# Two Fourier filters and two token MLPs on one core: the filter stage's last groups from one written list, more buffers and a sooner split

## The chip, the cores and the metric

The kernel runs on one core of one Trainium2 chip. Its time is the device time of one execution in microseconds (us); shown is the median of three runs. A core has five engines with an instruction stream each: TensorE (PE) for matmuls, VectorE (DVE), ScalarE (ACT) and GpSimd (POOL) for elementwise work, and SyncE (SP), which here only issues DMA transfers. An engine works through its own stream in order; engines wait for each other by semaphores. Matmuls write into PSUM, everything else lies in SBUF.

## The reference

Two kinds of layers alternate, A, B, A, B, each on the layer-normalised input and with a residual. A multiplies the 2-D spectrum with a complex filter, B is an MLP over the tokens:

```python
def A(x, w_r, w_i):                  # x: (1, 2048, 640)
    X = rfft2(x) * (w_r + 1j * w_i)  # (1, 2048, 321)
    return irfft2(X, s=(2048, 640))
def B(x, w1, b1, w2, b2):            # F = 1728
    h = layernorm(x)
    u = gelu(einsum("bsd,sf->bdf", h, w1) + b1)
    return (einsum("bdf,fs->bds", u, w2) + b2).transpose(0, 2, 1)

x = x + A(layernorm(x)); x = x + B(layernorm(x))
x = x + A(layernorm(x)); x = x + B(layernorm(x))
```

## The kernel before

The transforms are matmuls with tables of sines and cosines. To keep precision at f16 speed most operands are split into a high f16 part and a low f16 part (what the high one leaves over), and a product is three matmuls: high by high, high by low, low by high. So most stages have this shape: PE writes PSUM, ACT writes the high part from it, DVE or POOL the low part, PE reads both.

One pass over both layers is called a stage pair here; the program makes two of them. In each stand, in this order: a1, the filter stage (this case's subject); a2, the inverse transform of the rows, residual and the next layernorm; then the two products of the MLP, b1st and b2nd. What a1 hands to a2 is Y, split into Yh and Yl. A tile of a2 is 16 matmuls (`id_mm`), each of which reads rows of every group: the first two read Yh, the third Yl. ACT evicts the tile as "eh".

The filter stage works on 16 groups of columns, g = 0 to 15. A group passes through these steps; in the list of the change they go by the short names given here:

- d (`dstage`): 16 matmuls of 160 or 161 columns into a PSUM tile (24 for the first two groups); ph and pl: its high part (ACT) and low part (DVE).
- s (`s2stage`): 12 matmuls of 321 columns. For the last group it is done in three column blocks of 128, 128 and 65 columns, 12 matmuls each.
- ta, tb (`filtered`): two multiplies on DVE from that PSUM tile, with the filter's values w (a tile that SP loads per group) and a scale sx; each is 128 x 642.
- sa, sb (`sums`): the difference and the sum that finish the complex product, 128 x 321 each, on POOL.
- xh (ACT) and xl (POOL): the split of the product into f16; uh and ul (`twice`, ACT) copy 63 of its columns to columns 321 to 383, since the inverse transform reads a mirrored spectrum.
- i (`is2stage`): 36 matmuls of 64 rows and 128 columns in three column blocks, first those that read xh; Yh (ACT) and Yl (DVE, two instructions) split the result.

PSUM has four slots, and every `big()` takes the next one in turn; a group takes three (d, s, i). xh and xl lie in three buffers, `xs[g % 3]`. What runs when is written out by hand: all engine instructions go through a small wrapper (line 50, so every row of the profile has L50), which keeps them in program order on their engine while `self.pin` is set. DMAs on SP are not held this way; a scheduler places them.

The loop over g = 0 to 14 does d of group g + 1, i of group g - 3, s of group g, then xh, uh, xl of group g - 2, ta, tb, sa, sb of group g - 1, ph and pl of group g + 1, Yh and Yl of group g - 3, ul of group g - 2. Three other things are laid into it. `wsplit` splits the first weight tile of the MLP, in quarters: its high parts wh (ACT) at the end of g = 9 to 12, its low parts wl (DVE) behind pl at g = 10 to 13. The load of w of group g + 2 stands at the end of each g. And in the first of the two passes the bounds on the weights are worked out (`scan1`, `scale_b`, `scale1`), with two small matmuls by ones; each of them takes a PSUM slot of its own in `total`:

```python
        ps = at() if at else self.big()[:, 0, :n]
        self.PE.matmul(ps, self.ones, b, start=True, stop=True)
```

What is left of groups 13 to 15 after the loop is a sequence of its own. There the last group's product is worked on in two parts of columns, "a" (0 to 255) and "b" (256 to 320): ta15a, tb15a, ta15b, tb15b in a row on DVE; the sums of part a on POOL, of part b on DVE; xl15a and xl15b on DVE; the i of group 15 in two PSUM tiles. From its top:

```python
        h = self.big()
        for lt in range(3):
            s2mm(h, pp[k + 1], lt)
        xhi(k - 1, every, ta[k - 1])
        twice(k - 1, 0)
        xlo(k - 1, every, ta.pop(k - 1))
```

## Time and profile before

| | us |
|---|---|
| median of three runs | 1035.72 (1034.92 to 1037.0) |
| the profiled execution | 1035.4 |
| its span, first to last instruction | 1033.6 |
| PE busy | 988.2 (96%) |
| DVE busy | 723.8 (70%) |
| ACT busy | 571.1 (55%) |
| POOL busy | 264.1 (26%) |
| first filter stage, from 59.86 to 134.80: PE, DVE busy | 68.56, 62.34 |
| second filter stage, from 565.67 to 636.59: PE, DVE busy | 67.23, 59.06 |
| mean granted clock of TensorE | 0.977 |

How to read it: the span is cut from one profiled execution, and the rows of a timeline give the start, the duration of one instruction, its engine, the line, the operation, what it writes and reads with shapes and types, how many stand in a row, and in brackets for how long the engine had been idle before and which instruction released it. PE, DVE, ACT and POOL are engines, SPq is the queue that SP feeds. The granted clock is the share of full speed at which TensorE was allowed to run; 0.50 makes a matmul twice as long.

### The profile page before, as it was taken

The numbers are of one execution on the slowest core, as the hardware profiler recorded it, in microseconds if no ns is written. First come the engines' busy times: TensorE is split into PE (matmuls) and PEld (weight loads), VectorE is DVE, ScalarE is ACT, GpSimd is POOL, SyncE is SP. The second block draws the span as 40 slices with busy tenths as digits, with TensorE's granted clock in tenths as the row PEclk, the third lists the DMA queues.
The fourth block names the chain that finished last, engine by engine and source line by source line (L and its number), as shares of the span: only waits on it lengthen the run. The fifth ranks groups of instructions, "written<-read, shape, count | busy, mean of one in ns | idle before, by whom it ended". The sixth has DMA issues, their size and how long they took to land.

```text
span 1033.6 us, 20949 instructions
## 1 busy us (share of the span) xinstructions
PE 988.2 (96%) x8379; PEld 736.3 (71%) x8379; DVE 723.8 (70%) x1424; ACT 571.1 (55%) x874; POOL 264.1 (26%) x436
## 2 busy tenths in 40 slices
...
GB/s 226 276 181 173 101 161 220 210 84 93 80 78 75 71 238 153 135 130 123 124 64 95 195 132 120 199 186 197 129 84 82 72 107 78 140 153 174 163 44 52
DMA packets 55738, 139.48 MB, mean 135 GB/s; under 512 B 6461, under 2 KB 12249, under 8 KB 55641
## 3 DMA queue, kind: packets, MB, share of 16 engines
...
## 4 chain that ended last, share of the span: by engine, by line
PE 75%; DVE 10%; POOL 6%; ACT 4%; issue 3%; DMA 1%; SPq 0%; POOLq 0%; ACTq 0%; DVEq 0%
PE ps L50 75%; DVE st L50 2%; POOL ta L50 2%; DVE f L50 2%; POOL xt L50 1%; DVE xt L50 1%; DVE s1l L50 1%; DVE hl L50 1%; POOL xl L50 1%; ACT xh L50 1%; ACT eh L50 1%; DVE el L50 1%; POOL r L50 1%; DMA xt<-x 1%; POOL eo L50 1%
## 5 line engine op out<-in xcount | busy, mean ns | idle before, releaser
L50 PEld LDWEIGHTS <-wh 128*128 128x128 f16 x2992 | 289.7, 98 | 113.2 <-issue 1.7
L50 PEld LDWEIGHTS <-wl 128*128 128x128 f16 x1616 | 157.9, 98 | 62.2 <-DVE wl L50 0.7
L50 PE MATMUL ps<-hh,wh 128*128 128x320 f16 x896 | 186.6, 299 | 0.7 <-ACT hh L50 0.7
L50 PE MATMUL ps<-hl,wh 128*128 128x320 f16 x896 | 184.6, 299 | 0.0
L50 PE MATMUL ps<-hh,wl 128*128 128x320 f16 x832 | 171.5, 299 | 0.4 <-DVE wl L50 0.4
L50 DVE SCALAR_TENSOR_TENSOR wl<-raw,s,wh 128x1024 f16<-128x1024 f32 (+2 forms) x88 | 105.3, 1200 | 87.6 <-ACT wh L50 87.6
L50 PE MATMUL ps<-uh,wl 128*128 128x320 f16 x448 | 133.1, 299 | 0.0
L50 PE MATMUL ps<-ul,wh 128*128 128x320 f16 x448 | 133.0, 299 | 0.0
L50 ACT ACTIVATE wh<-raw,s 128x1024 f16<-128x1024 f32 (+2 forms) x92 | 94.7, 1047 | 69.0 <-PE ps L50 62.3
L50 PE MATMUL ps<-uh,wh 128*128 128x320 f16 x416 | 124.3, 299 | 0.0
L50 ACT ACTIVATE junk<-raw 128x896 bf16<-128x896 f32 (+1 forms) x60 | 59.6, 993 | 44.7 <-DMA raw<-w 44.5
L50 PE MATMUL ps<-tDi,Yh 128*128 128x322 f16 x320 | 73.3, 306 | 0.8 <-ACT Yh L50 0.8
L50 POOL TENSOR_TENSOR r<-v,mh 128x1 f32<-128x1 f32 x64 | 37.4, 584 | 133.2 <-DVE nm L50 122.8
L50 PE MATMUL ps<-u,wo 128*128 128x320 f16 x504 | 69.9, 299 | 0.0
L50 DVE TENSOR_TENSOR f<-eo 128x256 f32<-128x256 f32 (+1 forms) x124 | 39.0, 367 | 38.8 <-POOL eo L50 38.2
L50 PEld LDWEIGHTS <-wo 128*128 128x128 f16 x504 | 49.3, 98 | 19.1
L50 POOL TENSOR_TENSOR xt<-xt,ec 128x320 f32<-128x320 f32 x64 | 52.4, 840 | 40.8 <-DVE xt L50 40.5
L50 DVE BATCH_NORM_STATS2 st<-xt 128x6 f32<-128x320 f32 x126 | 55.2, 480 | 6.3 <-DMA xt<-x 5.3
L50 ACT ACTIVATE z<-xt,nb,r 128x640 f32<-128x640 f32 x31 | 28.5, 919 | 55.8 <-POOL z L50 43.5
L50 PE MATMUL ps<-ph,tS 128*128 128x321 f16 (+2 forms) x288 | 58.0, 286 | 0.1
L50 PE MATMUL ps<-tM,f 128*128 128x128 f32 x160 | 37.0, 396 | 22.1 <-DMA xt<-x 12.3
L50 PE MATMUL ps<-tDi,Yl 128*128 128x322 f16 x192 | 56.9, 305 | 1.1 <-DVE Yl L50 1.0
...
## 6 DMA issues: line engine op xcount, KB each, us to landing
...
```

The source lines that it names most:

```text
L50: i = f(*a, **k)
```

## The change

The steps of the loop become words, such as "ta12", and a function `do` carries one out. For g = 0 to 12 a generator `group` gives the words in the old order. All that is left of groups 11 to 15 from there on (what the loop did at g = 13 and 14, and the sequence behind it) is one list, `LAST`. A trailing "!" puts a sum on DVE, which without it is on POOL. The two sums of a product are apart now (`suma`, `sumb`), and so are ta and tb (`term`).

On PE, i of group 10 stands behind d of group 15 and s of group 14 now (before, behind d of group 14, ahead of s of group 13), and the last third of group 15's s, `s15b`, behind i of group 11, where it follows tb15a; sa14, sb15a and sa15b are on DVE, and the sums sb14, sa15a and sb15b and both xl of group 15 on POOL. Before, sa14, sb14 and both sums of part a were on POOL, both sums of part b and the two xl on DVE.

The x split has five buffers in place of three. The two small matmuls write into columns 400 and 402 of the second bank of the newest s tile, which the product doesn't use, and `scale1`'s last step goes from g = 9 to g = 8. `wsplit` begins one group sooner, at g = 8 with wh and at g = 9 with wl.

```diff
+NX = 5
+LAST = '''
+    d14 s13 xh11 uh11 ph14 ta12 tb12 xl11 d15 pl14 s14 ul11 ta13 ph15 i10 tb13 sa12 pl15 sb12 ta14 s15 xh12 sa13 sb13
+    tb14 xh13 sa14! uh13 ta15a i11 Yh10 xl12 tb15a xl13 Yl10 uh12 ul12 Yh11 sb14 sa15a s15b xh14 xl14 sb15a! ta15b
+    ul13 tb15b i12 sa15b! Yh12 Yl11 uh14 xh15a ul14 i13 Yl12 i14 sb15b xl15a Yh13 xh15b uh15 Yh14 Yl13 xl15b Yl14 i15a
+    ul15 Yh15a i15b Yh15b Yl15a Yl15b
+'''
...
-    def scale_b(self):
+    def scale_b(self, at=None):
 
         b = self.base
         sq = b.tile([128, 1, 1], F32, name="sqs")
         bsq = b.tile([128, NFT], F32, name="bsq")
         self.T.activation(bsq, self.b1, AF.Square, accum_out=sq[:, 0])
         yield
-        for ps in self.total(sq):
+        for ps in self.total(sq, at):
             yield
...
-        for i in range(3):
+        for i in range(NX):
...
-        def sums(tt, c, W=G):
+        def suma(tt, c, W=G):
 
             ta, tb = (q[:, :, c] for q in tt)
             W.tensor_tensor(ta[:, 0], ta[:, 0], tb[:, 1], op=ALU.subtract)
+
+        def sumb(tt, c, W=G):
+
+            ta, tb = (q[:, :, c] for q in tt)
             return W.tensor_tensor(ta[:, 1], tb[:, 0], ta[:, 1], op=ALU.add)
 
...
+        def term(g, i, c):
+
+            if i not in tt[g]:
+                tt[g][i] = self.t(p, [128, 2, NL], F32, "tatb"[2 * i:2 * i + 2], 3 - i)
+            filtered(tt[g][i][:, :, c], ps2[g][:, :, c], g, w[g][:, :, c], i)
 
...
-        for g in range(NG - 1):
-            q = psplit(dstage(g + 1))
+        tt = collections.defaultdict(dict)
+        part = {"": every, "a": slice(0, 256), "b": slice(256, NL)}
+        ltile = {"": slice(0, 3), "a": slice(0, 2), "b": slice(2, 3)}
+        dst = {}
+
+        def do(op):
+            name, g, c, dve = re.fullmatch(r"([a-zY]+)(\d+)([ab]?)(!?)", op).groups()
+            g, W = int(g), V if dve else G
+            pair = lambda: (tt[g][0], tt[g][1])
+            if name == "d":
+                dst[g] = dstage(g)
+            elif name == "ph":
+                dst[g] = psplit(dst[g])
+                next(dst[g])
+            elif name == "pl":
+                pp[g] = next(dst.pop(g))
+            elif name == "s" and g < NG - 1:
+                ps2[g] = s2stage(g, *pp.pop(g))
+            elif name == "s":
+                if not c:
+                    ps2[g] = self.big()
+                for lt in (2,) if c else (0, 1):
+                    s2mm(ps2[g], pp[g], lt)
...
+            elif name == "sb":
+                ins = sumb(pair(), part[c], W)
...
+            elif name == "i":
+                pv[g, c] = self.big()
+                for lt in range(3)[ltile[c]]:
+                    is2mm(pv[g, c], g, lt)
+            elif name == "Yh":
+                yhi(g, pv[g, c], ltile[c])
+            elif name == "Yl":
+                ylo(g, pv[g, c], ltile[c])
+
+        def group(g):
+            k = g - 1
+            yield f"d{g + 1}"
             if g > 2:
-                pv[g - 3] = is2stage(g - 3)
-            ps2[g] = s2stage(g, *pp.pop(g))
+                yield f"i{g - 3}"
+            yield f"s{g}"
+            if k > 0:
+                yield from (f"xh{k - 1}", f"uh{k - 1}", f"xl{k - 1}")
+            if k >= 0:
+                yield from (f"ta{k}", f"tb{k}", f"sa{k}", f"sb{k}")
+            yield from (f"ph{g + 1}", f"pl{g + 1}")
+            if g > 2:
+                yield from (f"Yh{g - 3}", f"Yl{g - 3}")
+            if k > 0:
+                yield f"ul{k - 1}"
+
+        spare = lambda c: lambda: ps2[max(ps2)][:, 1, c:c + 1]
+        for g in range(NG - 3):
+            for op in group(g):
+                do(op)
+                if op == "pl%d" % (g + 1) and 9 <= g < 13:
+                    self.wsplit(0, quarter(g - 9)[0], hi=False, part=quarter(g - 9)[1])
+                if op == "s0" and first:
+                    for _ in self.scale_x(p):
+                        pass
             i = g % NC
             if i:
                 stack(g + 3)
...
-            if k >= 0 and g + 2 < NG:
+            if g > 0 and g + 2 < NG:
                 w[g + 2] = wload(g + 2)
             if g == 3:
                 self.wload(0)
                 self.wopen(0)
             if first and g == 4:
-                sb = self.scale_b()
+                sb = self.scale_b(at=spare(400))
             if first and 4 <= g < 8:
                 next(sb)
             if first and g in (5, 6):
                 self.scan1(0, (g - 5,))
             if first and g == 7:
-                sc0 = self.scale1(0)
-            if first and 7 <= g < 10:
+                sc0 = self.scale1(0, at=spare(402))
                 next(sc0)
-            if 9 <= g < 13:
-                self.wsplit(0, quarter(g - 9)[0], lo=False, part=quarter(g - 9)[1])
-
-        k = NG - 2
-        parts = slice(0, 256), slice(256, NL)
...
+        g = NG - 3
+        w[g + 2] = wload(g + 2)
+        for op in LAST.split():
+            do(op)
```

The order of instructions is shown at three places of the second filter stage. First DVE, from the multiply of group 12 on. Before, ta_1181, ta_1189, ta_1194 and ta_1197 are groups 12 to 15, and ps1179 and ps1187 the i results of groups 10 and 11:

```order
L50 SCALAR_TENSOR_TENSOR ta_1181_8877<-ps1172_8773,sx_81,w_1160_8622 128x642
L50 SCALAR_TENSOR_TENSOR tb_1182_8878<-ps1172_8773,sx_81,w_1160_8622 128x642
L50 SCALAR_TENSOR_TENSOR pl_1184_8884<-ps1178_8807,ph_1183_8883 128x2x321
L50 SCALAR_TENSOR_TENSOR wl_1101_7999<-raw_1099_7996,s0_72,wh_1100_7998 128x512
L50 SCALAR_TENSOR_TENSOR Yl1061_7707<-ps1179_8824,Yh1061_7706 128x96x4 x2
L50 SCALAR_TENSOR_TENSOR ta_1189_8964<-ps1180_8861,sx_81,w_1169_8716 128x642
L50 SCALAR_TENSOR_TENSOR tb_1190_8965<-ps1180_8861,sx_81,w_1169_8716 128x642
L50 SCALAR_TENSOR_TENSOR pl_1192_8971<-ps1186_8894,ph_1191_8970 128x2x321
L50 SCALAR_TENSOR_TENSOR Yl1061_7707<-ps1187_8911,Yh1061_7706 128x96x4 x2
L50 SCALAR_TENSOR_TENSOR ta_1194_9018<-ps1188_8948,sx_81,w_1177_8804 128x642
L50 SCALAR_TENSOR_TENSOR tb_1195_9019<-ps1188_8948,sx_81,w_1177_8804 128x642
```

After, ta_1181, ta_1185, ta_1190 and ta_1193 are groups 12 to 15:

```order
L59 SCALAR_TENSOR_TENSOR ta_1181_8851<-ps1170_8781,sx_81,w_1158_8630 128x642
L59 SCALAR_TENSOR_TENSOR tb_1182_8853<-ps1170_8781,sx_81,w_1158_8630 128x642
L59 SCALAR_TENSOR_TENSOR pl_1180_8849<-ps1177_8816,ph_1179_8848 128x2x321
L59 SCALAR_TENSOR_TENSOR ta_1185_8888<-ps1178_8833,sx_81,w_1167_8724 128x642
L59 SCALAR_TENSOR_TENSOR tb_1189_8930<-ps1178_8833,sx_81,w_1167_8724 128x642
L59 SCALAR_TENSOR_TENSOR pl_1187_8891<-ps1183_8856,ph_1186_8890 128x2x321
L59 SCALAR_TENSOR_TENSOR ta_1190_8935<-ps1184_8874,sx_81,w_1175_8812 128x642
L59 SCALAR_TENSOR_TENSOR tb_1192_8965<-ps1184_8874,sx_81,w_1175_8812 128x642
L59 TENSOR_TENSOR ta_1190_8935<-ta_1190_8935,tb_1192_8965 128x321
L59 SCALAR_TENSOR_TENSOR ta_1193_8970<-ps1191_8937,sx_81,w_1176_8814 128x2x256
L59 SCALAR_TENSOR_TENSOR tb_1195_9011<-ps1191_8937,sx_81,w_1176_8814 128x2x256
```

The last quarter of wl is gone from between the multiplies, Yl of group 10 (ps1188) has moved behind tb15a, and the first sum of group 14 (TENSOR_TENSOR) is new among them.

Then ACT and POOL in the end of the stage. ACT before, where xh2 is the split of group 14 and xh0 that of group 15 (128x2x256 is part a, 128x2x65 part b, 128x2x63 a copy uh or ul):

```order
L50 ACTIVATE xh2_1062_7717<-ta_1194_9018 128x2x321
L50 ACTIVATE xh2_1062_7717<-xh2_1062_7717 128x2x63
L50 ACTIVATE Yh1061_7706<-ps1196_9025 128x2x96x4
L50 ACTIVATE xh0_1062_7713<-ta_1197_9062 128x2x256
L50 ACTIVATE xh0_1062_7713<-ta_1197_9062 128x2x65
L50 ACTIVATE xh0_1062_7713<-xh0_1062_7713 128x2x63
L50 ACTIVATE xl2_1062_7718<-xl2_1062_7718 128x2x63
L50 ACTIVATE xl0_1062_7714<-xl0_1062_7714 128x2x63
L50 ACTIVATE Yh1061_7706<-ps1199_9075 128x2x96x4
L50 ACTIVATE Yh1061_7706<-ps1200_9122 128x2x96x4
```

After, where xh4 is group 14 and xh0 group 15, and xl3 group 13:

```order
L59 ACTIVATE xh4_1060_7723<-ta_1190_8935 128x2x321
L59 ACTIVATE xl3_1060_7722<-xl3_1060_7722 128x2x63
L59 ACTIVATE Yh1059_7708<-ps1196_9039 128x2x96x4
L59 ACTIVATE xh4_1060_7723<-xh4_1060_7723 128x2x63
L59 ACTIVATE xh0_1060_7715<-ta_1193_8970 128x2x256
L59 ACTIVATE xl4_1060_7724<-xl4_1060_7724 128x2x63
L59 ACTIVATE Yh1059_7708<-ps1197_9083 128x2x96x4
L59 ACTIVATE xh0_1060_7715<-ta_1193_8970 128x2x65
L59 ACTIVATE xh0_1060_7715<-xh0_1060_7715 128x2x63
L59 ACTIVATE Yh1059_7708<-ps1198_9122 128x2x96x4
L59 ACTIVATE xl0_1060_7716<-xl0_1060_7716 128x2x63
```

The copy ul of group 13 and Yh of group 12 now stand between xh14 and its copy, ul14 (xl4) stands between the two parts of xh15, and part b of it behind Yh of group 13. POOL at the same place, before (from the sums of group 13; xl2 is group 14):

```order
L50 TENSOR_TENSOR ta_1189_8964<-ta_1189_8964,tb_1190_8965 128x321
L50 TENSOR_TENSOR ta_1189_8964<-tb_1190_8965,ta_1189_8964 128x321
L50 TENSOR_TENSOR xl1_1062_7716<-ta_1189_8964,xh1_1062_7715 128x2x321
L50 TENSOR_TENSOR ta_1194_9018<-ta_1194_9018,tb_1195_9019 128x321
L50 TENSOR_TENSOR ta_1194_9018<-tb_1195_9019,ta_1194_9018 128x321
L50 TENSOR_TENSOR ta_1197_9062<-ta_1197_9062,tb_1198_9063 128x256
L50 TENSOR_TENSOR ta_1197_9062<-tb_1198_9063,ta_1197_9062 128x256
L50 TENSOR_TENSOR xl2_1062_7718<-ta_1194_9018,xh2_1062_7717 128x2x321
```

After (xl2 to xl4 are groups 12 to 14, xl0 is group 15):

```order
L59 TENSOR_TENSOR ta_1185_8888<-ta_1185_8888,tb_1189_8930 128x321
L59 TENSOR_TENSOR ta_1185_8888<-tb_1189_8930,ta_1185_8888 128x321
L59 TENSOR_TENSOR xl2_1060_7720<-ta_1181_8851,xh2_1060_7719 128x2x321
L59 TENSOR_TENSOR xl3_1060_7722<-ta_1185_8888,xh3_1060_7721 128x2x321
L59 TENSOR_TENSOR ta_1190_8935<-tb_1192_8965,ta_1190_8935 128x321
L59 TENSOR_TENSOR ta_1193_8970<-ta_1193_8970,tb_1195_9011 128x256
L59 TENSOR_TENSOR xl4_1060_7724<-ta_1190_8935,xh4_1060_7723 128x2x321
L59 TENSOR_TENSOR ta_1193_8970<-tb_1195_9011,ta_1193_8970 128x65
L59 TENSOR_TENSOR xl0_1060_7716<-ta_1193_8970,xh0_1060_7715 128x2x256
L59 TENSOR_TENSOR xl0_1060_7716<-ta_1193_8970,xh0_1060_7715 128x2x65
```

The sums of group 13 stand ahead of xl of group 12; the first sum of group 14 and the second of part a are gone, and the second sum of part b and the two xl of group 15 are new.

Last SP, where w_1169, w_1177 and w_1185 are the filter tiles of groups 13 to 15 and raw the halves of an MLP weight tile. Before:

```order
L476 DMA w_1169_8716<-w 128x642
L821 DMA raw_1226_9377<-w1 128x1024
L476 DMA w_1177_8804<-w 128x642
L476 DMA w_1185_8892<-w 128x642
L821 DMA raw_1227_9379<-w1 128x1024
L705 DMA xt0_1205_9236<-x2_0_99 128x640
```

After, where they are w_1167, w_1175 and w_1176:

```order
L834 DMA raw_1224_9383<-w1 128x1024
L485 DMA w_1167_8724<-w 128x642
L485 DMA w_1175_8812<-w 128x642
L834 DMA raw_1225_9385<-w1 128x1024
L485 DMA w_1176_8814<-w 128x642
L718 DMA xt0_1203_9242<-x2_0_99 128x640
```

Each half of raw stands one load sooner, so that w of group 15 is behind the second one, and xt of a2 behind it.

105 lines of the change are left out of this document (26 added, 79 removed).

## The prediction

> **What bounds the kernel now.** I read the page first, then the timeline of PE at the end of each of the two filter stages, then busy time and clock by stretches.
>
> ```profile
> PE 988.2 (96%) x8379; PEld 736.3 (71%) x8379; DVE 723.8 (70%) x1424; ACT 571.1 (55%) x874; POOL 264.1 (26%) x436
> PE 75%; DVE 10%; POOL 6%; ACT 4%; issue 3%; DMA 1%; SPq 0%; POOLq 0%; ACTq 0%; DVEq 0%
> ```
>
> PE is the bound: 96% busy and 75% of the chain that ended last. The change alters no matmul, so it can only give or take time where PE waits or runs at a low clock. In the filter stages that is nearly all at their ends. The timeline of PE there, first stage and second stage:
>
> ```profile
> 129.16 0.28 PE L50 MATMUL ps<-tI,xh 64*128 64x128 f16 x4 [1.12 <-ACT xh L50]
> 130.94 0.29 PE L50 MATMUL ps<-tI,xl 64*128 64x128 f16 x2 [1.50 <-POOL xt L50]
> 135.59 0.45 PE L50 MATMUL ps<-tDi,Yl 128*128 128x322 f16 x1
> ...
> 631.83 0.29 PE L50 MATMUL ps<-tI,xh 64*128 64x128 f16 x4 [1.12 <-ACT xh L50]
> 633.61 0.23 PE L50 MATMUL ps<-tI,xl 64*128 64x128 f16 x2 [1.49 <-POOL xt L50]
> 638.05 0.31 PE L50 MATMUL ps<-tDi,Yl 128*128 128x322 f16 x1 [1.01 <-DVE Yl L50]
> ```
>
> PE waits there for the split of group 14, then for Y of the last groups. The clock falls too. Busy time by stretches of 3.41 us (busy and count of each engine, then granted clock, DMA share, GB/s):
>
> ```profile
> 20.57:23.98 3.41, 1.91 (x10) 1.34 (x10) 3.38 (x9) 1.79 (x4) 3.25 (x9) 1.00 0.47 131
> 58.12:61.53 3.41, 2.07 (x22) 1.68 (x22) 2.35 (x4) 2.79 (x7) 0.00 (x0) 1.00 0.78 273
> 126.38:129.80 3.42, 1.65 (x48) 1.13 (x42) 2.58 (x6) 1.72 (x4) 3.42 (x6) 1.00 0.16 20
> 129.80:133.21 3.41, 2.27 (x44) 2.28 (x46) 2.38 (x6) 2.91 (x8) 1.75 (x7) 0.50 0.81 276
> 631.56:634.97 3.41, 1.64 (x54) 1.48 (x56) 1.72 (x5) 3.08 (x9) 2.66 (x9) 1.00 0.07 9
> 634.97:638.38 3.41, 1.61 (x31) 0.91 (x26) 3.26 (x9) 1.84 (x4) 0.00 (x0) 1.00 0.53 148
> 638.38:641.80 3.42, 3.42 (x15) 1.90 (x14) 0.01 (x1) 0.05 (x1) 0.00 (x0) 0.50 0.02 5
> ```
>
> After a stretch with 1.65 us of PE work the clock is 0.50, after 1.61 too; after 1.64 once it is not. So near half idle, PE is slowed for the next stretch.
>
> **The list of the last groups.** I measure each end from the first multiply (ta) of group 12 on DVE to PE's first matmul that reads Yl. DVE, first stage, then the same multiply of the second:
>
> ```profile
> 117.06 0.87 DVE L50 SCALAR_TENSOR_TENSOR ta<-ps,sx,w 128x642 f32<-128x642 f32 x1
> 118.65 0.82 DVE L50 SCALAR_TENSOR_TENSOR pl<-ps,ph 128x642 f16<-128x642 f32 x1
> 119.39 0.96 DVE L50 SCALAR_TENSOR_TENSOR wl<-raw,s,wh 128x512 f16<-128x512 f32 x1
> 120.27 1.01 DVE L50 SCALAR_TENSOR_TENSOR Yl<-ps,Yh 128x384 f16<-128x384 f32 x2
> ...
> 126.69 0.73 DVE L50 SCALAR_TENSOR_TENSOR tb<-ps,sx,w 128x512 f32<-128x512 f32 x1
> 127.35 0.34 DVE L50 SCALAR_TENSOR_TENSOR ta<-ps,sx,w 128x130 f32<-128x130 f32 x1
> 127.98 0.43 DVE L50 TENSOR_TENSOR ta<-ta,tb 128x65 f32<-128x65 f32 x1
> 128.33 0.67 DVE L50 TENSOR_TENSOR ta<-tb,ta 128x65 f32<-128x65 f32 x1
> ...
> 619.74 0.87 DVE L50 SCALAR_TENSOR_TENSOR ta<-ps,sx,w 128x642 f32<-128x642 f32 x1
> ```
>
> Before, an end takes 135.59 - 117.06 = 18.53 us in the first stage and 638.05 - 619.74 = 18.31 in the second. For after I follow the list by start-to-start times: ta and tb together 1.59, pl 0.74, wl 0.88, tb on 512 columns 0.66; what has no successor here starts the next some 0.08 ahead of its end (tb 0.73 long, 0.66 apart), so a Yl pair 0.93. PE, ACT and POOL have these:
>
> ```profile
> 619.93 0.29 PE L50 MATMUL ps<-tI,xh 64*128 64x128 f16 x4
> 621.04 0.31 PE L50 MATMUL ps<-ph,tS 128*128 128x321 f16 x1
> 622.70 0.30 PE L50 MATMUL ps<-tD,s1h 128*128 128x160 f16 x2
> 623.93 0.29 PE L50 MATMUL ps<-tI,xh 64*128 64x128 f16 x4
> ...
> 129.35 0.79 ACT L50 ACTIVATE Yh<-ps 128x768 f16<-128x768 f32 x1
> 130.04 0.82 ACT L50 ACTIVATE xh<-ta 128x512 f16<-128x512 f32 x2
> 130.89 0.31 ACT L50 ACTIVATE xh<-xh 128x126 f16<-128x126 f16 x1
> ...
> 127.57 0.76 POOL L50 TENSOR_TENSOR ta<-tb,ta 128x321 f32<-128x321 f32 x1
> 129.46 1.42 POOL L50 TENSOR_TENSOR xl<-ta,xh 128x642 f16<-128x642 f32 x1
> ```
>
> An i step is 1.11 on PE, s 1.66, d 1.23. From group 12's ta (time 0) PE does s13, d15, s14, i10 and two thirds of s15, 24 matmuls of 128 columns (12 of 321 take 1.66; in proportion 1.3): 1.66 + 1.23 + 1.66 + 1.11 + 1.3, with 0.3 for start and end 7.3. DVE has its eight operations (ta, tb, pl, ta, tb, pl, ta, tb) issued by 6.25, so group 15's ta starts at 7.3, its tb ends at 7.3 + 0.66 + 0.73 = 8.7. Behind it stand the last third of s15, which writes the same PSUM tile (0.4), i12 (1.11) and 0.3 of starts and ends: Yh12 at 10.5. From there ACT is full: Yh12 0.69, uh14 0.22 (0.31 less the overlap), xh15a 0.5 (the 0.82 of both parts less the small one), ul14 0.22, Yh13 0.69, xh15b 0.34, uh15 0.22, Yh14 0.79 = 3.7, so 14.2; on DVE Yl14 0.93 and the two halves of Yl15a, some 0.75, and PE reads Yl at 16.0. POOL keeps ahead: sa13 starts with the end of tb13 at 4.0; two sums 1.5, xl12 and xl13 2.8, two sums 1.4, xh14 of ACT 0.75, xl14 1.4 give 11.9 at the latest, before the ul14 that reads it (11.9), and xl15a, b by 13.6, before ul15 (14.2).
>
> What the trace does not show is a DVE sum over 321 or 256 columns beside POOL. The nearest rows are the 65-column sums: 0.43 and 0.67 for a seventh of the data of the 0.73 row, so they waited 0.3 to 0.5 each for the POOL sum at 127.57. Low end: no wait on any engine, then DVE's own work from ta12 to Yl15a counts, 6 multiplies 4.8, 2 pl 1.5, the parts of group 15 1.9, five Yl pairs 4.65, Yl15a 0.75 and three sums of some 0.4: 14.8. High end: each of the three sums waits out a whole xl of 1.42; 4.3 less the 0.6 free before ta15a and some 0.4 between the Yl pairs, 19.3. I take 16.3, by the rows of 0.43 and 0.67. Gain of the list: 2.2 in the first end, 2.0 in the second; by the bounds from 3.7 to a loss of 1.0 each.
>
> The rule that speaks against the moved sums is in the Trainium skill, SBUF — State Buffer, "Who interferes with whom": a DVE instruction with two SBUF inputs and a GpSimd instruction that reads SBUF exclude each other, and the second waits until the first is done. The two sum rows agree; taken at its worst it is the high end, taken by what was left of POOL's sum it is my 16.3.
>
> **The MLP tile's split one group sooner.** Its wl (0.88, four of them) go from groups 10-13 to 9-12. The one of group 13 stood inside the 18.5, so its going is counted. Now four stand ahead of group 12's ta, not three. The one that is new at group 9 finds idle time on DVE there:
>
> ```profile
> 605.97 1.02 DVE L50 SCALAR_TENSOR_TENSOR Yl<-ps,Yh 128x384 f16<-128x384 f32 x2 [0.39 <-ACT Yh L50]
> ```
>
> The cost is 0 (idle time there and in the groups just before takes it all) to 0.5 (0.88 less the 0.39): I take 0.2 in the second stage, nearer the low end since DVE waited for ACT there, which the same step will not do longer. In the first the next part pays it. On SP, group 15's w now stands behind the second raw half; it is issued when tb12 ends (1.7), must be there at 7.3, and only a landing later than 5.6 us would delay ta15a and everything behind it on DVE. A load of that size was issued at 58.68 and released its reader at 61.60:
>
> ```profile
> 58.68 0.33 SPq L212 DMA_DIRECT2D w<-w  x1
> 61.60 0.74 ACT L50 ACTIVATE jw<-w 128x642 bf16<-128x642 f32 x1 [0.21 <-DMA w<-w]
> ```
>
> With 2.9 us I cost it at nothing. The xt loads behind it are first read after the second eh (16.3 + 2.1 + 2.2 = 20.6 on this scale, below), by then long landed even if they wait for POOL's last xl at 13.6.
>
> **Scale matmuls in spare columns, five buffers.** Before, the small matmul takes one of four PSUM slots and PE waits for it:
>
> ```profile
> 90.65 0.30 PE L50 MATMUL ps<-tD,s1h 128*128 128x160 f16 x2 [0.42 <-DVE pl L50]
> ```
>
> 0.4, first stage only. DVE is nearly full from group 9 on and eats what PE gains, so I set it against the extra wl of that stage and count nothing more; the ends are 0.4 and 0. The five buffers hide no wait of the old order (no xh waits for PE in these rows); they allow the new one: 0 by themselves.
>
> **The clock.** From the first Yl matmul to the first eh are 14 matmuls:
>
> ```profile
> 138.21 0.80 ACT L50 ACTIVATE eh<-ps,cxe 128x644 fp32r<-128x644 f32 x1 [3.04 <-PE ps L50]
> 140.40 0.80 ACT L50 ACTIVATE eh<-ps,cxe 128x644 fp32r<-128x644 f32 x1 [1.39 <-PE ps L50]
> 641.75 0.80 ACT L50 ACTIVATE eh<-ps,cxe 128x644 fp32r<-128x644 f32 x1 [4.94 <-PE ps L50]
> ```
>
> At full clock 16 take 140.40 - 138.21 = 2.19, so 14 need 2.1; before they took 2.62 and 3.70. The difference, 0.5 and 1.6, comes back if the clock stays up. In my schedule PE's waits after time 13 are four pieces of 0.2 to 0.5, some 1.4 in a stretch, which leaves 2.0 of 3.41 busy, between the 1.91 that lost the clock and the 2.07 that did not. I take the nearer, 2.07. The page TensorE: Matmul & The Clock Gate of the Trainium skill ("What's actually happening") has the clock fall only after an idle window of some 3.4 us; by that it would not fall here and the 2.1 were sure. The trace disagrees, it fell with 1.65 busy, so the loss stays a rival.
>
> **Sum.** First end 2.2 + 0.5, second 2.0 - 0.2 + 1.6: 6.1 us. The stage behind starts sooner and runs PE-bound, so it carries on. The profiled execution took 1035.4, so 1029.3 by its own scale; the median of the three runs is 0.3 above it, 1035.7 - 6.1 = 1029.6.
>
> **Rivals.** B, the clock falls all the same at one end or both: a stretch at half rate costs 3.41 / 2 = 1.7, so 1031.3 or 1033.0. For it 1.91, against it 2.07. C, the ends get shorter by 1 us or less each, since any late step of a fixed list holds all behind it on ACT, and the clock stays as before: 1033.7 to 1035.7. For it: ACT has no slack from 10.5 on. Against: POOL and DVE each come some 0.3 to 0.6 early there. D, slower: the three DVE sums wait out whole xl operations; it decides from 2.2 us of waiting beyond the slack, and at the high end of 19.3 loses 0.8 and 1.0 + 0.2 with the clock unchanged: 1037.7. Against it: the two sums in the trace waited for no more than the rest of one POOL sum. That the spare columns free nothing is also possible: it costs the 0.4 set against the wl.
>
> **How the numbers follow.** A, my sum, 0.48, B 0.30, C 0.12, D 0.06; 0.04 is left for what I do not see, half of it faster. 0.2% is 2.07 us, about what a measurement of this kernel can tell from no change, so faster begins at 1033.65: A, B and that half make 0.80, C and a quarter of the rest 0.13, D and the last quarter 0.07. The range runs from 1027.2 (four fifths of the way to the low end of 14.8, which is 1.5 under my 16.3 in each end) to 1034.0, past B with both ends and into C; most of C and D are left out.
>
> **What would show it.** After, PE's idle before xl of group 14 should be under 0.7, its first Yl matmul 16.3 us after group 12's ta, the clock 1.00 in both ends, DVE's 321-column sum under 0.9, the 0.42 at the fifth group gone. Wrong I am if a DVE sum takes over 1.4, if ta of group 15 waits for a load, or if half-clock stretches stay.

## The result, and the profile after

| | before | after |
|---|---|---|
| median, us | 1035.72 (1034.27 to 1037.0, 5 runs) | 1029.19 (1027.76 to 1031.17, 5 runs) |
| profiled execution, span | 1035.4, 1033.6 | 1028.95, 1027.2 |
| PE, DVE, ACT, POOL busy | 988.2, 723.8, 571.1, 264.1 | 986.3, 725.5, 571.2, 265.7 |
| mean granted clock | 0.977 | 0.980 |

The ratio is 0.9937, 95% interval 0.9921 to 0.9953, so the change saves 6.5 us (4.9 to 8.2). A second measurement on one chip, beside three of the experiments, gave 1030.41 against 1035.96, ratio 0.9945 (0.9930 to 0.9959). The engines' work is nearly the same. The wrapper is line 59 of the new kernel, so its rows have L59. From the page of after, its lines of busy time and of the chain that ended last:

```profile
PE 986.3 (96%) x8379; PEld 735.7 (72%) x8379; DVE 725.5 (71%) x1422; ACT 571.2 (56%) x874; POOL 265.7 (26%) x438
PE 76%; DVE 13%; POOL 3%; issue 3%; DMA 2%; ACT 2%; SPq 0%; POOLq 0%; DVEq 0%; ACTq 0%
```

POOL's share of the chain fell from 6% to 3% and DVE's rose from 10% to 13%. The timeline of PE at the ends of the two filter stages of after, rows with idle time ahead of them:

```profile
126.84 0.19 PE L59 MATMUL ps<-ph,tS 128*128 128x65 f16 x1 [0.82 <-DVE tb L59]
129.78 0.23 PE L59 MATMUL ps<-tI,xl 64*128 64x128 f16 x2 [0.18 <-POOL xl L59]
131.34 0.23 PE L59 MATMUL ps<-tI,xl 64*128 64x128 f16 x2 [0.27 <-POOL xl L59]
132.43 0.23 PE L59 MATMUL ps<-tI,xl 64*128 64x128 f16 x2 [0.25 <-ACT xl L59]
134.23 0.31 PE L59 MATMUL ps<-tDi,Yl 128*128 128x322 f16 x1 [0.86 <-DVE Yl L59]
...
633.19 0.31 PE L59 MATMUL ps<-tDi,Yl 128*128 128x322 f16 x1 [0.80 <-DVE Yl L59]
```

The waits of 1.12 and 1.50 us for the split of group 14 are gone; pieces of 0.2 to 0.9 are left. DVE of after, from group 12's ta on in the first stage, and the same multiply in the second:

```profile
118.23 0.87 DVE L59 SCALAR_TENSOR_TENSOR ta<-ps,sx,w 128x642 f32<-128x642 f32 x1
...
124.57 0.90 DVE L59 TENSOR_TENSOR ta<-ta,tb 128x321 f32<-128x321 f32 x1
125.39 0.74 DVE L59 SCALAR_TENSOR_TENSOR ta<-ps,sx,w 128x512 f32<-128x512 f32 x1
126.05 0.74 DVE L59 SCALAR_TENSOR_TENSOR tb<-ps,sx,w 128x512 f32<-128x512 f32 x1
126.71 1.01 DVE L59 SCALAR_TENSOR_TENSOR Yl<-ps,Yh 128x384 f16<-128x384 f32 x2
127.64 0.68 DVE L59 TENSOR_TENSOR ta<-tb,ta 128x256 f32<-128x256 f32 x1
128.24 0.34 DVE L59 SCALAR_TENSOR_TENSOR ta<-ps,sx,w 128x130 f32<-128x130 f32 x1
128.50 0.34 DVE L59 SCALAR_TENSOR_TENSOR tb<-ps,sx,w 128x130 f32<-128x130 f32 x1
128.88 0.92 DVE L59 TENSOR_TENSOR ta<-ta,tb 128x65 f32<-128x65 f32 x1
129.72 4.85 DVE L59 SCALAR_TENSOR_TENSOR Yl<-ps,Yh 128x384 f16<-128x384 f32 x12
...
617.18 0.87 DVE L59 SCALAR_TENSOR_TENSOR ta<-ps,sx,w 128x642 f32<-128x642 f32 x1
```

The ends, from this ta to the first matmul that reads Yl, are 134.23 - 118.23 = 16.00 and 633.19 - 617.18 = 16.01 us, after 18.53 and 18.31. DVE has no idle row in either. ACT of after there:

```profile
128.52 0.81 ACT L59 ACTIVATE Yh<-ps 128x768 f16<-128x768 f32 x1
...
131.39 0.79 ACT L59 ACTIVATE Yh<-ps 128x768 f16<-128x768 f32 x1
...
136.36 0.80 ACT L59 ACTIVATE eh<-ps,cxe 128x644 fp32r<-128x644 f32 x1 [3.11 <-PE ps L59]
635.32 0.80 ACT L59 ACTIVATE eh<-ps,cxe 128x644 fp32r<-128x644 f32 x1 [3.04 <-PE ps L59]
```

From the first Yl matmul to eh are 2.13 us in both stages (2.62 and 3.70 before). Busy time by stretches of the clock in after (busy and count of PE, PEld, DVE, ACT, POOL, then granted clock):

```profile
65.79:69.20 3.41, 1.62 (x15) 1.00 (x14) 2.08 (x12) 0.00 (x0) 0.00 (x0) 1.00 0.41 80
69.20:72.61 3.41, 3.41 (x19) 2.38 (x18) 3.04 (x4) 0.71 (x1) 0.93 (x2) 0.50 0.46 127
...
130.63:134.04 3.41, 2.13 (x46) 1.21 (x40) 3.41 (x9) 2.59 (x7) 1.79 (x8) 1.00 0.39 108
...
632.40:635.82 3.42, 2.63 (x20) 1.86 (x21) 1.13 (x5) 0.50 (x1) 0.57 (x1) 1.00 0.59 147
```

At the ends the clock stays at 1.00. At the beginning of the first stage it fell once, from 69.20 on. Before, it had not, as its stretches there show:

```profile
64.94:68.36 3.42, 2.80 (x28) 2.04 (x26) 1.53 (x9) 0.00 (x0) 0.00 (x0) 1.00 0.45 112
68.36:71.77 3.41, 2.15 (x20) 1.57 (x19) 3.34 (x8) 0.71 (x1) 0.34 (x1) 1.00 0.36 105
```

PE's waits there are alike (0.62 and 1.26 before; 0.62 and 1.17, the latter for a DMA, after), but before they lay in two stretches and here in one. That put group 12's ta of this execution some 1.1 us later, counted from the stage's first matmul (58.20; 57.06 in the kernel with three buffers below, whose first stage had no such stretch, and 57.20 before), and hides a part of the first stage's gain. So the experiments are read by spans inside a stage, and by the ends above all.

### The profile page after: what moved, and what is told of

Same layout as the page of the kernel before. It is cut to its first block, busy times and chain, and to the rows that moved or that the text cites. A ratio compares the mean times of both kernels' runs of the same rounds, so it can differ in the third digit from the quotient of the medians.

```text
span 1027.2 us, 20943 instructions
## 1 busy us (share of the span) xinstructions
PE 986.3 (96%) x8379; PEld 735.7 (72%) x8379; DVE 725.5 (71%) x1422; ACT 571.2 (56%) x874; POOL 265.7 (26%) x438
## 3 DMA queue, kind: packets, MB, share of 16 engines
q8 instruction: 66, 1.08, 0.4%
## 4 chain that ended last, share of the span: by engine, by line
PE 76%; DVE 13%; POOL 3%; issue 3%; DMA 2%; ACT 2%; SPq 0%; POOLq 0%; DVEq 0%; ACTq 0%
PE ps L59 76%; DVE st L59 2%; POOL xt L59 2%; DVE xt L59 2%; DVE f L59 1%; DVE Yl L59 1%; DVE s1l L59 1%; DVE hl L59 1%; DVE ta L59 1%; ACT eh L59 1%; DVE el L59 1%; DMA rest<-s1l 1%; POOL r L59 1%; DVE tb L59 1%; DMA stk<-rest 1%
## 5 line engine op out<-in xcount | busy, mean ns | idle before, releaser
L59 PEld LDWEIGHTS <-wh 128*128 128x128 f16 x2992 | 289.7, 98 | 113.4 <-issue 1.8
L59 PEld LDWEIGHTS <-wl 128*128 128x128 f16 x1616 | 157.9, 98 | 62.2 <-DVE wl L59 0.9
L59 PE MATMUL ps<-hh,wh 128*128 128x320 f16 x896 | 186.6, 299 | 0.7 <-ACT hh L59 0.7
L59 PE MATMUL ps<-hl,wh 128*128 128x320 f16 x896 | 184.7, 299 | 0.0
L59 PE MATMUL ps<-hh,wl 128*128 128x320 f16 x832 | 171.4, 299 | 0.6 <-DVE wl L59 0.6
L59 DVE SCALAR_TENSOR_TENSOR wl<-raw,s,wh 128x1024 f16<-128x1024 f32 (+2 forms) x88 | 105.4, 1202 | 87.4 <-ACT wh L59 87.3
L59 PE MATMUL ps<-uh,wl 128*128 128x320 f16 x448 | 133.1, 299 | 0.0
L59 PE MATMUL ps<-ul,wh 128*128 128x320 f16 x448 | 133.1, 299 | 0.0
L59 ACT ACTIVATE wh<-raw,s 128x1024 f16<-128x1024 f32 (+2 forms) x92 | 94.7, 1047 | 68.4 <-PE ps L59 61.6
L59 PE MATMUL ps<-uh,wh 128*128 128x320 f16 x416 | 124.3, 299 | 0.0
L59 ACT ACTIVATE junk<-raw 128x896 bf16<-128x896 f32 (+1 forms) x60 | 59.6, 994 | 46.5 <-DMA raw<-w 46.4
L59 POOL TENSOR_TENSOR r<-v,mh 128x1 f32<-128x1 f32 x64 | 37.4, 584 | 132.2 <-DVE nm L59 122.6
L59 PE MATMUL ps<-tDi,Yh 128*128 128x322 f16 x320 | 71.3, 300 | 0.2
L59 PE MATMUL ps<-u,wo 128*128 128x320 f16 x504 | 69.9, 299 | 0.0
L59 DVE TENSOR_TENSOR f<-eo 128x256 f32<-128x256 f32 (+1 forms) x124 | 39.1, 368 | 38.8 <-POOL eo L59 38.1
L59 PEld LDWEIGHTS <-wo 128*128 128x128 f16 x504 | 49.3, 98 | 19.1
L59 POOL TENSOR_TENSOR xt<-xt,ec 128x320 f32<-128x320 f32 x64 | 52.4, 841 | 32.8 <-DVE xt L59 32.6
L59 PE MATMUL ps<-ph,tS 128*128 128x321 f16 (+2 forms) x288 | 59.6, 289 | 1.3 <-DVE tb L59 1.3
L59 ACT ACTIVATE z<-xt,nb,r 128x640 f32<-128x640 f32 x31 | 28.5, 919 | 55.8 <-POOL z L59 43.5
L59 DVE BATCH_NORM_STATS2 st<-xt 128x6 f32<-128x320 f32 x126 | 55.3, 481 | 5.7 <-DMA xt<-x 4.6
L59 PE MATMUL ps<-tM,f 128*128 128x128 f32 x160 | 39.5, 426 | 19.8 <-DVE f L59 19.8
L59 POOL TENSOR_TENSOR eo<-z 128x320 f32<-128x320 f32 x62 | 53.3, 880 | 17.1 <-ACT z L59 15.1
```

Of the source, the lines that this page charges most:

```text
L59: i = f(*a, **k)
```

## The experiments

All ends below are from group 12's ta to the first Yl matmul.

### The old order in the new kernel

The list was written in the order of before, with the splits of group 15 and the sums where they stood; buffers, spare columns and the sooner MLP split stayed.

```diff
-    d14 s13 xh11 uh11 ph14 ta12 tb12 xl11 d15 pl14 s14 ul11 ta13 ph15 i10 tb13 sa12 pl15 sb12 ta14 s15 xh12 sa13 sb13
...
+    d14 i10 s13 xh11 uh11 xl11 ta12 tb12 sa12 sb12 ph14 pl14 Yh10 Yl10 ul11
+    d15 i11 s14 xh12 uh12 xl12 ta13 tb13 sa13 sb13 ph15 pl15 Yh11 Yl11 ul12
+    s15 s15b xh13 uh13 xl13 ta14 tb14 sa14 sb14 ul13 i12 ta15a tb15a sa15a sb15a ta15b tb15b sa15b! sb15b! xh14 uh14 Yh12 i13
+    xh15a xl15a! xh15b xl15b! uh15 xl14 Yl12 ul14 ul15 i14 Yh13 Yl13 i15a Yh14 Yl14 i15b Yh15a Yl15a Yh15b Yl15b
```

> The changed kernel with its last groups in the old order and the sums and splits on the engines where they stood before; five buffers, spare columns and the sooner MLP split stay. Ends are measured from group 12's ta to PE's first matmul that reads Yl (before 18.53 and 18.31 us, after 16.00 and 16.01). My theory (the order of the list shortens the ends): only the missing wl of 0.88 us is left of the gain, ends of 17.5 to 17.8, the clock at 0.50 again in at least one end, 1034 us. Rival, the sooner split alone did it: ends of 16.3 or less, no half clock, 1029 to 1030 us. Rival, five buffers did it: the same 1029 to 1030 us.

Measured: 1033.08 us (1031.33 to 1035.76) against 1036.15, ratio 0.9972 (0.9960 to 0.9983). PE's timeline of that kernel:

```profile
129.16 0.29 PE L59 MATMUL ps<-tI,xh 64*128 64x128 f16 x4 [1.12 <-ACT xh L59]
130.94 0.29 PE L59 MATMUL ps<-tI,xl 64*128 64x128 f16 x2 [1.49 <-POOL xl L59]
...
135.59 0.31 PE L59 MATMUL ps<-tDi,Yl 128*128 128x322 f16 x1 [0.34 <-DVE Yl L59]
...
632.23 0.23 PE L59 MATMUL ps<-tI,xl 64*128 64x128 f16 x2 [1.50 <-POOL xt L59]
```

Both waits are back, and the clock is at 0.50 from 130.9 to 134.3 and from 632.7 to 636.1. The ends are 18.07 and 17.86, so some 2.0 of the 2.5 and 1.9 of the 2.3 us come from the order of the list and the places of the sums. I had expected 17.5 to 17.8: of the missing wl of 0.88 only 0.46 shows in this order. The sooner split and the buffers alone do not make the new end. From the first Yl matmul to eh are 2.13 us in both ends here, though the clock fell in both: the half-clock stretches were over before that matmul (134.3 and 135.59, 636.1 and 636.66). So what a fall costs hangs on where its stretch lies, and the 2.62 and 3.70 of before are those of one execution.

### The MLP split at its old groups

```diff
-                if op == "pl%d" % (g + 1) and 9 <= g < 13:
-                    self.wsplit(0, quarter(g - 9)[0], hi=False, part=quarter(g - 9)[1])
+                if op == "pl%d" % (g + 1) and 10 <= g < 13:
+                    self.wsplit(0, quarter(g - 10)[0], hi=False, part=quarter(g - 10)[1])
...
-            if 8 <= g < 12:
-                self.wsplit(0, quarter(g - 8)[0], lo=False, part=quarter(g - 8)[1])
+            if 9 <= g < 13:
+                self.wsplit(0, quarter(g - 9)[0], lo=False, part=quarter(g - 9)[1])
...
             do(op)
+            if op == "pl14":
+                self.wsplit(0, quarter(3)[0], hi=False, part=quarter(3)[1])
```

> The changed kernel with the MLP tile's split back at its old groups, so that its last wl (0.88 us) stands behind pl of group 14 in the list. My theory: DVE has no idle time in the new end, so both ends get longer by 0.7 to 0.9 us, to 16.7 to 16.9, group 12's ta comes 0.1 to 0.3 sooner, the clock stays 1.00 in the ends, 1030 to 1031 us. Rival, the sooner split is what shortens the ends: 18 us and more, half clock again, 1034 to 1036 us. Rival, DVE is not the limit: ends of 16.0 to 16.2 us, time as after.

Measured: 1029.46 us (1028.57 to 1032.3) against 1036.15, ratio 0.9945 (0.9926 to 0.9963); ends 16.89 and 16.88. Each end is 0.88 longer, a whole wl, as for a DVE without idle time. But what the wl costs ahead of group 12 has to be set against it. From group 8's ta to eh are 35.8 us in the second stage, 35.1 with the sooner split (the kernel with three buffers, below, whose clock was the same there). So the sooner split saves 0.7 in the second stage. In the first the figures are 34.9 and 35.2, but this execution's first stage began in a half-clock stretch and its group 8 was still 1.4 us late, so what the split does there stays open. The time can't tell the kernel from after.

### The clock alone: spare matmuls in PE's waits

The kernel before, with matmuls that fill PE's waits at the ends and change nothing else.

```diff
+        def fill(n):
+            for _ in range(n):
+                mm(hs[:, 1, 400:], self.tS2[:, 0, 0, 0], self.tS2[:, 0, 0, 1, :112], start=True, stop=True)
...
+        fill(20)
         pv[k] = is2stage(k)
...
+                    if (g, lt, ri, k) == (NG - 2, 0, 0, 2):
+                        fill(27)
...
+                    if j == 0 and lt == 0 and ty == 0:
+                        fill(ps, 14)
...
                         mm(ps[:, ty, :322], a[0], b[1], start=False, stop=False)
+                        fill(ps, 18)
```

> The kernel before, with spare matmuls of 112 columns into unused PSUM columns in the four waits of PE at each end (20 ahead of group 14's i, 27 before its first matmul that reads xl, 14 before the first and 18 before the third matmul of a2); they change no result. It asks for the clock alone. My theory (PE's idle time makes the clock fall): no half-clock stretch from 120 to 146 and from 622 to 646 us, from the first Yl matmul to eh 2.0 to 2.2 us in both ends where it was 2.62 and 3.70, ends themselves as before within 0.3, time 2.1 us less, 1033.6. Rival, the clock falls for another reason: half clock stays, 1035.7 or, with the extra matmuls at half clock, up to 1037.

Measured: 1036.15 us (1034.93 to 1037.21) against 1036.15, ratio 0.9997 (0.9988 to 1.0007). The clock was at 1.00 through both ends and Yl to eh took 2.12, but the ends grew to 19.02 and 19.03: the spare matmuls of a2, 0.9 us of them between Yh and Yl, ended after Yl was ready. The mechanism was right and the price not measured, so it was tried with fewer, 19, 26, 12 and 8:

```diff
-        fill(20)
+        fill(19)
...
-                        fill(27)
+                        fill(26)
...
-                        fill(ps, 14)
+                        fill(ps, 12)
...
-                        fill(ps, 18)
+                        fill(ps, 8)
```

> The kernel before with spare matmuls in PE's waits at the ends, fewer than in the first try, which asked PE to finish 18 of them after Yl was ready (19, 26, 12 and 8 in place of 20, 27, 14 and 18). My theory (the clock's fall costs 0.5 and 1.6 us): ends of 18.3 to 18.6 us, 2.1 us from Yl to eh in both, 1.5 to 2.2 us less than before. Rival (the clock is no loss by itself, since others then set the time): the same as before within 0.5 us.

Measured: 1034.33 us (1033.73 to 1036.2) against 1035.96, ratio 0.9986 (0.9977 to 0.9994), 1.5 us less (0.6 to 2.4). Stretches of 3.40 us through its two ends:

```profile
125.00:128.40 3.40, 3.12 (x94) 2.79 (x91) 3.37 (x8) 1.08 (x4) 3.11 (x4) 1.00 0.02 5
128.40:131.80 3.40, 3.23 (x73) 2.64 (x69) 1.71 (x4) 3.06 (x9) 2.95 (x9) 1.00 0.61 146
131.80:135.20 3.40, 2.46 (x59) 2.10 (x58) 3.25 (x9) 2.36 (x4) 0.00 (x0) 1.00 0.99 348
633.00:636.40 3.40, 2.67 (x74) 2.26 (x71) 2.53 (x6) 3.10 (x8) 1.59 (x7) 1.00 0.32 71
636.40:639.80 3.40, 3.08 (x48) 2.43 (x45) 2.35 (x7) 0.99 (x3) 0.00 (x0) 1.00 0.25 90
```

PE's idle time makes the clock fall, and matmuls without any use prevent it. Yl to eh is 2.12 in both; ends are 18.42 and 18.43, since the second end gains nothing ahead of Yl. Only spare matmuls were added, so this is the part of the change's gain that the clock can bring by itself.

### Three buffers

```diff
-NX = 5
+NX = 3
```

> The changed kernel with three buffers of the split product, as before, and all else as after. My theory (the buffers hide no wait of their own): ends of 16.0 to 16.3 us, 1029 to 1030. Rival, the new order lives on the five buffers: xh of groups 13 to 15 waits for i of groups 10 to 12, ends of 17 us and more, 1031 to 1033 us.

Measured: 1028.57 us in one run; ends 132.94 - 116.93 = 16.01 and 632.93 - 616.92 = 16.01, the same as with five. The five buffers do nothing here, neither by themselves nor for the list. Its first stage had no half-clock stretch inside: from the first matmul to eh 75.20 us, against 78.35 before.

### The three sums back on POOL

```diff
-    tb14 xh13 sa14! uh13 ta15a i11 Yh10 xl12 tb15a xl13 Yl10 uh12 ul12 Yh11 sb14 sa15a s15b xh14 xl14 sb15a! ta15b
-    ul13 tb15b i12 sa15b! Yh12 Yl11 uh14 xh15a ul14 i13 Yl12 i14 sb15b xl15a Yh13 xh15b uh15 Yh14 Yl13 xl15b Yl14 i15a
+    tb14 xh13 sa14 uh13 ta15a i11 Yh10 xl12 tb15a xl13 Yl10 uh12 ul12 Yh11 sb14 sa15a s15b xh14 xl14 sb15a ta15b
+    ul13 tb15b i12 sa15b Yh12 Yl11 uh14 xh15a ul14 i13 Yl12 i14 sb15b xl15a Yh13 xh15b uh15 Yh14 Yl13 xl15b Yl14 i15a
```

> The changed kernel with its three sums on DVE (sa14, sb15a, sa15b) back on POOL, at the same places of the list. My theory (POOL's chain to xl of groups 14 and 15 is what the moved sums shorten): DVE is rid of 0.90 + 0.68 + 0.92 us, POOL has two sums of 0.75 and a small one more ahead of xl of groups 14 and 15, ends of 17.4 to 18.2 us, 1032 to 1034 us. Rival (the two engines shut each other out, so a sum on DVE costs what it saves on POOL): ends of 16.2 us or less, 1028 to 1030 us.

Measured: 1033.28 us (1032.31 to 1034.12) against 1036.96, ratio 0.9967 (0.9958 to 0.9976); ends 18.01 and 18.05. Nearly the whole gain of the ends is lost. The clock stayed at 1.00 through both, so Yl to eh is 2.13 here too. POOL and then DVE of its second end:

```profile
626.44 0.75 POOL L59 TENSOR_TENSOR ta<-ta,tb 128x321 f32<-128x321 f32 x1 [0.91 <-DVE tb L59]
627.15 2.78 POOL L59 TENSOR_TENSOR xl<-ta,xh 128x642 f16<-128x642 f32 x2
```

```profile
628.60 0.75 DVE L59 SCALAR_TENSOR_TENSOR ta<-ps,sx,w 128x512 f32<-128x512 f32 x1 [2.24 <-POOL xl L59]
```

It is not only POOL's chain to the splits of groups 14 and 15. The tile ta has three buffers, so ta15a writes where ta12 was, and xl12 on POOL is its last reader; a fourth buffer wasn't tried. With sa14 on POOL, ahead of xl12 in the list, POOL waits 0.91 us for tb14, xl12 comes later, and DVE stands idle for 2.24 us. With sa14 on DVE neither engine waits there. I had not seen this wait. The new order with the sums on POOL (18.01 and 18.05) is no shorter than the old order with the sums where they stood (18.07 and 17.86; sa15b was on DVE there too), so it gains only together with the sums on DVE. The old order with sa14 and sb15a on DVE wasn't tried, nor the three sums one by one.

### The three sums left out

```diff
-    tb14 xh13 sa14! uh13 ta15a i11 Yh10 xl12 tb15a xl13 Yl10 uh12 ul12 Yh11 sb14 sa15a s15b xh14 xl14 sb15a! ta15b
-    ul13 tb15b i12 sa15b! Yh12 Yl11 uh14 xh15a ul14 i13 Yl12 i14 sb15b xl15a Yh13 xh15b uh15 Yh14 Yl13 xl15b Yl14 i15a
+    tb14 xh13 uh13 ta15a i11 Yh10 xl12 tb15a xl13 Yl10 uh12 ul12 Yh11 sb14 sa15a s15b xh14 xl14 ta15b
+    ul13 tb15b i12 Yh12 Yl11 uh14 xh15a ul14 i13 Yl12 i14 sb15b xl15a Yh13 xh15b uh15 Yh14 Yl13 xl15b Yl14 i15a
```

> The changed kernel without the three sums on DVE (they are left out, so groups 14 and 15 come out wrong); it asks what bounds the new end. My theory (ACT is full from Yh of group 12 on): ends of 15.6 to 16.0 us although DVE has 2.5 us less to do. Rival (DVE's own work is the limit): ends of 13.7 to 14.5 us.

Measured: 1030.16 us in one run; ends 134.52 - 119.00 = 15.52 and 634.22 - 618.05 = 16.17. DVE of its first end:

```profile
125.94 0.75 DVE L59 SCALAR_TENSOR_TENSOR ta<-ps,sx,w 128x512 f32<-128x512 f32 x1 [0.63 <-POOL xl L59]
...
129.93 1.02 DVE L59 SCALAR_TENSOR_TENSOR Yl<-ps,Yh 128x384 f16<-128x384 f32 x2 [0.20 <-ACT Yh L59]
131.54 1.02 DVE L59 SCALAR_TENSOR_TENSOR Yl<-ps,Yh 128x384 f16<-128x384 f32 x2 [0.59 <-ACT Yh L59]
132.78 2.08 DVE L59 SCALAR_TENSOR_TENSOR Yl<-ps,Yh 128x384 f16<-128x384 f32 x6 [0.22 <-ACT Yh L59]
```

DVE is rid of 2.5 us of work and idles instead, first for the buffer of ta12, then for ACT's Yh. So DVE bounds the new end by a hair only: the wl of 0.88 put back on it lengthened each end in full, 2.5 us taken off it shortened the first by 0.48. Right behind it come ACT, which has no slack from Yh of group 12 on, and the buffer of ta12, in whose wait the sum sa14 lies. The second end is longer than after's 16.01 because its zero came sooner: group 12's ta is 16.56 us behind group 8's, 16.93 in after, and there ta15a waited for PE (the first two thirds of s15 end at 625.55, ta15a starts at 625.64). From group 8's ta to eh the second stage took 34.86, 35.07 in after.

### Scale matmuls in slots of their own

```diff
-                sb = self.scale_b(at=spare(400))
+                sb = self.scale_b(at=None)
...
-                sc0 = self.scale1(0, at=spare(402))
+                sc0 = self.scale1(0, at=None)
```

> The changed kernel with the two scale matmuls in PSUM slots of their own, as before. My theory: PE's wait of 0.42 us before the fifth group's d comes back, group 12's ta in the first stage is 0.3 to 0.7 us later after the stage's first matmul than with the spare columns (57.06 us in the kernel with three buffers, whose stage had no half-clock stretch), ends of 16.0. Rival (the wait is absorbed by DVE's work ahead of group 12): ta at 57.0 to 57.2.

Measured: 1029.56 us in one run, ends 16.00 and 16.02. The wait is back in PE's timeline:

```profile
91.17 0.30 PE L59 MATMUL ps<-tD,s1h 128*128 128x160 f16 x2 [0.46 <-DVE pl L59]
```

Group 12's ta comes 57.39 us after the stage's first matmul, 57.06 with spare columns and three buffers: 0.33, the expected size, seen once. But the four other kernels here with spare columns whose first stage had no half-clock stretch ahead of that ta (the old list and the three tries below) have 57.11 to 57.26. So the columns are worth some 0.1 to 0.3 us, and the rival isn't out.

### Is there a better one?

PE's wait of 0.82 us in the first end of after is for tb15a, since the last third of group 15's s writes the same PSUM tile. Directly behind the first two thirds that third needs some 0.4 us of PE. With sa15b on POOL beside it:

```diff
-    d14 s13 xh11 uh11 ph14 ta12 tb12 xl11 d15 pl14 s14 ul11 ta13 ph15 i10 tb13 sa12 pl15 sb12 ta14 s15 xh12 sa13 sb13
-    tb14 xh13 sa14! uh13 ta15a i11 Yh10 xl12 tb15a xl13 Yl10 uh12 ul12 Yh11 sb14 sa15a s15b xh14 xl14 sb15a! ta15b
-    ul13 tb15b i12 sa15b! Yh12 Yl11 uh14 xh15a ul14 i13 Yl12 i14 sb15b xl15a Yh13 xh15b uh15 Yh14 Yl13 xl15b Yl14 i15a
+    d14 s13 xh11 uh11 ph14 ta12 tb12 xl11 d15 pl14 s14 ul11 ta13 ph15 i10 tb13 sa12 pl15 sb12 ta14 s15 s15b xh12 sa13 sb13
+    tb14 xh13 sa14! uh13 ta15a i11 Yh10 xl12 tb15a xl13 Yl10 uh12 ul12 Yh11 sb14 sa15a xh14 xl14 sb15a! ta15b
+    ul13 tb15b i12 sa15b Yh12 Yl11 uh14 xh15a ul14 i13 Yl12 i14 sb15b xl15a Yh13 xh15b uh15 Yh14 Yl13 xl15b Yl14 i15a
```

> The changed kernel with the last third of group 15's s directly behind the first two and sa15b on POOL, nothing else. My theory: ends of 15.5 to 15.7 us as in the try before, so 0.8 us less than after, 1028 to 1029 us. Rival (the shorter ends are eaten further on): the time of after within 0.2 us.

Measured: 1027.79 us (1026.12 to 1031.28) against 1035.96, ratio 0.9923 (0.9908 to 0.9939); ends 15.55 and 16.24. In the two tries below, which have the same list, the ends are 15.54 and 15.65, and 15.54 and 15.66; the 16.24 holds a wait of 0.98 us on PE that the trace puts to no engine. After, on the same chip, had 16.00 and 16.48 with such a wait of 1.11. So the ends are shorter by some 0.4 us each, and it has the lowest median here of kernels run more than once, but its interval and that of after (0.9930 to 0.9959) overlap: the time alone doesn't tell them apart. Its two edits weren't tried apart.

Other half-clock stretches lie at the beginning of the second stage, one to three of them. There PE waits some 4 us for the split of the last row of the transform before. The first try to fill that wait had the spare matmuls behind it:

```diff
+            q = self.big()
+            if i == 0:
+                for _ in range(64):
+                    self.PE.matmul(q[:, 1, :128], self.ones, self.ones, start=True, stop=True)
+            q = q[:, 0, :n]
```

> A try at a better kernel, three edits on the changed one: the last third of group 15's s directly behind the first two (no wait for tb15a, 0.82 and 0.45 us of PE), sa15b on POOL (its 0.92 us on DVE was mostly waiting), and 64 spare matmuls by ones in the 4.36 us in which PE waits ahead of the second filter stage, so that the clock doesn't fall there. My theory: ends of 15.3 to 15.9 us, no half-clock stretch between 556 and 572 us, where there were one to three of 3.41 us, 1026 to 1028 us. Rival (the chain behind PE sets the time and the clock costs nothing there): 1028.5 to 1030 us.

Measured: 1033.19 us (1031.97 to 1035.8) against 1036.96, ratio 0.9973 (0.9962 to 0.9983), ends 15.54 and 15.65. The wait of 4.06 us was still there, the clock was at half from 555.6 to 562.4, and the spare matmuls ran in PE's way from 559.16 on, for 5.3 us (not the 7 that the next expectation has) and partly at half clock. Then ahead of it:

```diff
     def a0_s1(self, j, fh, fl, warm=0):
         ps = self.big().rearrange("p a b -> p (a b)")
+        for _ in range(warm):
+            self.PE.matmul(ps[:, 768:896], self.ones, self.ones, start=True, stop=True)
...
-            ps.append((k, self.a0_s1(k, *self.a0_lo(f, fh))))
+            ps.append((k, self.a0_s1(k, *self.a0_lo(f, fh), warm=0 if ps else 60)))
```

> The try at a better kernel again, with the spare matmuls (60) moved ahead of the first matmul of PE's long wait; in the try before they stood behind it, ran at half clock and took 7 us. My theory: ends of 15.5 to 15.7 us, no half-clock stretch between 556 and 572 us, the second stage's first matmul as early as after or earlier, 1025.5 to 1028 us. Rival (the clock there is not on the path): as the next kernel without them, 1028 to 1029 us.

Measured: 1029.88 us (1028.9 to 1031.09) against 1035.96, ratio 0.9939 (0.9927 to 0.9951). PE's timeline and stretches of that kernel:

```profile
554.21 3.51 PE L59 MATMUL ps<-ones 128*128 128x128 bf16 x60
558.96 0.23 PE L59 MATMUL ps<-tM,fl 128*128 128x128 f16 x1 [1.12 <-DVE fl L59]
...
570.11 0.23 PE L59 MATMUL ps<-tD,stk 96*128 96x160 f16 x1 [2.69 <-DMA stk<-rest]
```

```profile
557.40:560.82 3.42, 2.17 (x36) 1.82 (x33) 2.58 (x8) 1.94 (x4) 0.00 (x0) 1.00 0.35 99
...
567.64:571.06 3.42, 0.95 (x14) 0.98 (x15) 1.29 (x2) 0.00 (x0) 1.46 (x2) 1.00 0.42 93
571.06:574.47 3.41, 3.41 (x18) 2.02 (x16) 0.86 (x2) 1.65 (x3) 1.41 (x1) 0.51 0.68 198
```

The stretches from 556 to 567 are at full clock now, but PE only arrives sooner at a matmul that waits for a DMA (stk), 2.69 us where after waited 1.08, and that wait lets the clock fall in the next stretch. In this execution the transfer set the time, not the clock. That is not so in each: in the same list without spare matmuls PE came to this matmul at 569.37, after three half-clock stretches, and did not wait; its transfer `rest<-s1l` was issued at 562.16, 562.28 here, but the load that needs it went out at 565.76, 567.56 here. Why it was 1.7 us slower isn't shown, nor what the full clock is worth when it is not. This try gains nothing over the same list without it.

### The changed kernel once more

> The changed kernel itself, on the same chip as the three others, for comparison: 1028.5 to 1030 us, ends of 16.0 us. A half-clock stretch of 3.41 us at the beginning of the first stage, as its first profile showed from 69.2 us on, would not come again if it was a matter of where the stretches fall; if the change causes it, it comes again.

Measured: 1030.41 us (1028.81 to 1031.36) against 1035.96; ends 16.00 and, with the wait of 1.11 us put to no engine, 16.48. No half-clock stretch at 69 us this time, but one from 60.0 to 63.4. PE's waits there:

```profile
67.75 0.39 PE L59 MATMUL ps<-eye,xb 16*128 16x16 f32 x2 [0.62 <-DVE xb L59]
70.79 0.30 PE L59 MATMUL ps<-pl,tS 128*128 128x321 f16 x1 [1.26 <-DVE pl L59]
```

They are those of before (0.62 and 1.26), so the stretch of 69.20 in the first profile goes with where the stretches fell, and perhaps with a DMA that landed late, and not with the list.

## Why the prediction held

Forecast 1029.6 us, measured 1029.19; forecast a gain of 6.1 us, measured 6.5 (4.9 to 8.2). The steps came out near enough; that the medians agree within 0.4 us is also luck, since half-clock stretches at the beginnings of the stages, which the forecast doesn't have, shifted one stage by some 1 us between executions. Step by step:

- **The list's end.** 16.3 us were forecast, 16.00 and 16.01 measured. On the scale from group 12's ta: ta15a at 7.3, measured 125.39 - 118.23 = 7.16; the end of tb15a at 8.7, measured 8.56; Yh12 at 10.5, measured 10.29; the end of ACT's Yh14 at 14.2, measured 131.39 + 0.79 - 118.23 = 13.95. Each is 0.1 to 0.3 early, so the gains are 2.5 and 2.3 and not 2.2 and 2.0.
- **What holds ta15a.** Here the number was right partly by luck and the reason incomplete. I let PE's s15 set it. In the first end of after the first two thirds of s15 are done at 124.91, 0.48 us ahead of ta15a, which DVE comes to straight from sa14, a sum that my 7.3 did not have in its way; in the second they are done at 624.31 and ta15a starts at 624.41, so there PE and sa14 tie. With the sum taken off DVE, ta15a waits for xl12 on POOL (0.63 and, with all three sums on POOL, 2.24), because ta has three buffers. The three sums on DVE, which I had only as a risk, are needed for 2.0 of the ends' gain.
- **The price of the DVE sums.** Bounds of no wait and of a whole xl each, taken by the rows of 0.43 and 0.67. Measured 0.90, 0.68 and 0.92 long (the first where I had named under 0.9 as the sign); the 65-column sum, the smallest, takes longest, while POOL runs xl from 128.30 for 1.42. That last one ends at 129.80, just behind the xl at 129.72. A sum of 256 columns took 0.41 to 0.42 in the second ends of the three tries, begun while POOL was idle, and 0.68 and 0.62 in after, begun beside a POOL sum, so the two engines do hold each other up, as the Trainium skill's page SBUF — State Buffer ("Who interferes with whom") has it. It costs little here: without the sums the ends are 15.52 and 16.17. Rival D is out.
- **The split one group sooner.** Its 0.2 us in the second stage agree with 0.88 less 0.7. In the first I set it against the 0.4 of the spare columns; what it costs there stayed open; the spare columns give 0.1 to 0.3.
- **The five buffers.** Nothing was forecast for them alone, which is so. That the new order needs them was wrong: with three the ends are the same.
- **The clock.** 0.5 and 1.6 us were forecast, 2.0 of 3.41 us busy in the last stretch. Measured 2.13 busy in that stretch, the clock at 1.00, and Yl to eh shorter by 0.49 and 1.57. Spare matmuls alone brought 1.5 us (0.6 to 2.4) of the 2.1, so the size is right within what was measured. The price in the sum came from one execution, though, and its 2.1 for 14 matmuls does not follow from 2.19 for 16, which gives 1.9. Rival B is out in the profiled ends, and not by luck alone: if a window of 3.41 us is moved over after's first end, the least work in it is 1.94 us, and about a tenth of its possible positions have under 2.0; in the first end of before the least is 0.79, and some such window lies in it wherever the stretches fall. These runs are also against the rule of the Trainium skill's page TensorE: Matmul & The Clock Gate ("What's actually happening"), a fall only after an idle window: the clock fell after stretches with 1.62 and 0.95 us of work, and stayed after 2.13 and 2.17.
- **The sum.** By the three-buffer kernel, whose first stage is free of a half-clock stretch as that of before, the first stage is 78.35 - 75.20 = 3.15 us shorter to eh (forecast 2.7), and the second, with three such stretches at its beginning in both, 76.08 - 72.50 = 3.58 (forecast 3.4).
